# Splitting the last output row of an MLP over two stores, and dropping an early load of gelu's table

## The chip, the cores and the metric

The kernel runs on one core of a Trainium2 chip. A time is the device time of one execution in microseconds. A core has a matrix engine (TensorE, PE in the profile; PEld is its loading of weights), a vector engine (VectorE, DVE), an activation engine (ScalarE, ACT), a general engine (GpSimd, POOL) and a queue engine (SyncE, SP). They run side by side and wait for one another through semaphores. TensorE writes its sums to a memory of its own, PSUM, with eight banks; VectorE and ScalarE move results from there to the on-chip memory SBUF. DMA transfers move data between SBUF and the chip's main memory.

## The reference

The input has 2048 positions of 448 channels. A block computes a long convolution over positions with gates, by Fourier transforms of 4096 points. Then an MLP mixes over the positions, not the channels. Cut to what matters:

```
kv = shift(k) * v
y  = irfft(rfft(pad(kv)) * rfft(pad(ssm_k)))[:S] + kv * ssm_D
h  = x + layernorm(x) * y
z  = layernorm(layernorm(h))
u  = gelu(einsum("bsd,sf->bdf", z, w1) + b1)     # 448 x 1792
out = h + transpose(einsum("bdf,fs->bds", u, w2) + b2)
```

gelu is the tanh form. `w1` is 2048 x 1792 and `w2` is 1792 x 2048, in bf16.

## The kernel before, in words

Position 16 q + r is held in partition q at row r, so that all 2048 positions are 16 rows (R = 16) of 128 partitions by 448 channels. One SBUF tensor, `arena`, holds everything, and one PSUM tensor, `ps`.

The transforms are matmuls with tables of sines. These tables are made in `emit_tables`. VectorE and GpSimd make integer phases, and ScalarE turns them into sines: once 2048 elements a partition for each half of the table `E` (the activation at L823, two times, the first half of the table rows and then the second), and once 384 elements for small factors (L837). At the start a one-element sine (L759) brings sine's table of the activation function into ScalarE. At L851 a one-element gelu reads the small factors' place as a dependence, writes to a scratch column, and has no reader. The compiler puts a load of the function's table (ACT_TABLE_LOAD) ahead of each activation whose function isn't in the table loaded. There are four such loads in the program: ahead of L759 (sine), of L851 (gelu), of the second activation at L823 (sine), and of the first gelu of the MLP at L1270. Between the sines and after them ScalarE also copies sums out of PSUM (L712, L713, L1019).

The stages that follow are, by line: transposes of k and of the filter (L934, L989), the shift of k as matmuls (L953) with the product with v on VectorE (L959), the first stage of both transforms (L1009), its evacuation (L1017, L1019) and a shuffle by DMA (L1025), the second stage (L1044), the products (L1077), the two inverse stages (L1089, L1180), and the gates and both norms (L1187 to L1235).

`emit_mlp` is the MLP. The first layer has 14 groups of 16 matmuls (L1280 for groups 0 to 6, L1290 for 7 to 13), each group followed by a gelu on ScalarE (L1270) that writes `G`, 14 x 448 channels. The second layer has one group for each row r: 14 matmuls with the weights of positions 16 q + r (so the 128 weights of a matmul are 16 elements apart in SBUF) and the 448 columns of `G` (L1300), then a sum of the result, the bias and h on VectorE into `X` (L1304). Stores to the output are issued by SyncE: for rows 0 to 13 in pairs (L1308), for rows 14 and 15 alone (L1311). The table sets the order of the rows: row 14 comes third, row 6 last but one, row 15 last.

TensorE also runs matmuls without a reader, which fill idle time (L979, and L1123 in `emit_warm`). Eight of those stand at the end of its order.

The order of instructions is worked out when the program is built. Each operation is registered with what it reads and writes, an estimated duration and a due time (table `WHEN`). A list scheduler then plays the engines forward: each engine takes the ready operation of the earliest due time, and with equal due times that with the longest way to the end. It also deals out PSUM banks. Each engine then runs its instructions in the order found. Row 15 of the second layer and its sum and store have one due time.

Of the kernel before, what the change touches and what calls it, by code (L numbers as in the profile page):

```python
# [6 lines left out]
ACT = mybir.ActivationFunctionType  # L7
ALU = mybir.AluOpType
# [128 lines left out]
class _Sched:  # L137
# [51 lines left out]
    def op(self, W, fn, r=(), w=(), br=(), bw=(), n=0, kind=None, est=None, dmab=None, keng=16, rate=None, after=(), safter=(), mode=0):  # L189
        if (self.tag, self.t0) != self.step:  # L190
            self.step = (self.tag, self.t0)
            self.count[self.tag] = self.count.get(self.tag, -1) + 1
        o = _Op()
        o.id = len(self.ops)
        o.engs = W if isinstance(W, tuple) else (W,)
        o.eng = None
        o.fn = fn
        o.is_dma = dmab is not None
        o.nbytes = dmab or 0
        o.keng = keng  # L200
        o.lat = 2000.0 + o.nbytes / (22.0 * keng) if o.is_dma else 0.0
        if o.is_dma:
            o.est = {e: (585.0 if e == "pool" else 700.0 if keng == 8 else 460.0) for e in o.engs}
        elif est is not None:
            o.est = dict(est) if isinstance(est, dict) else {e: est for e in o.engs}
        else:
            o.est = {e: self.est_of(e, n, kind) for e in o.engs}
        o.ev = None
        o.mode = mode
        o.t0 = WHEN[self.tag][self.count[self.tag]]  # L210
        if len(o.engs) > 1:
            k = self.flex.get(self.tag, 0)
            self.flex[self.tag] = k + 1
            o.engs = {"a": ("act",), "d": ("dve",), "f": o.engs}[WHERE[self.tag][k]]
        o.rate = rate or (217.0 if keng == 8 else 425.0)
        o.tag = self.tag
        o.acq = []
        o.bufs = []
        o.extra = []
        preds = set(after)  # L220
        spreds = set(safter)
        for spec in r:
            for c in self._cells(spec):
                preds.update(c.w)
                c.r.append(o.id)
        for spec in w:
            g = spec[2] if len(spec) > 2 else None
            for c in self._cells(spec):
                rd = [x for x in c.r if x != o.id]
                if g is not None and c.g == g and not rd:  # L230
                    preds.update(c.gb)
                    c.w.append(o.id)
                else:
                    base = rd if rd else list(c.w)
                    preds.update(base)
                    c.w = [o.id]
                    c.r = []
                    c.g = g
                    c.gb = base
        for b in br:  # L240
            if len(self.ops) and all(self.ops[x].engs == ("pe",) for x in b.writers):
                preds.add(b.writers[-1])
            else:
                preds.update(b.writers)
            b.readers.append(o.id)
            o.bufs.append(b)
            b.users.append(o.id)
        for b in bw:
            if not b.writers:
                o.acq.append(b)  # L250
            else:
                spreds.add(b.writers[-1])
            b.writers.append(o.id)
            o.bufs.append(b)
            b.users.append(o.id)
        preds.discard(o.id)
        spreds -= preds
        o.preds = sorted(preds)
        o.spreds = sorted(spreds)
        self.ops.append(o)  # L260
        return o.id
# [304 lines left out]
def _build(nc, A_q, A_k, A_v, A_shift_k, A_ssm_k, A_ssm_D, B_w1, B_b1, B_w2, B_b2, out):  # L566
# [5 lines left out]
    Bsz, S, D = A_q.shape  # L572
    F = B_w1.shape[1]
    assert Bsz == 1 and S == 2048 and D == 448 and F == 1792 and A_shift_k.shape[-1] == 4
    R = 16
    NFC = F // 128
    EPS = 1e-5
    DB = 2 * D
# [9 lines left out]
    o2d = out[0].rearrange("(q r) d -> q r d", r=R)  # L588
# [15 lines left out]
    o_W2 = (o_TK, o_TU)  # L604
    o_TZ = 132736
    o_TT = o_TZ
    o_WR = 161408
    o_G = o_WR
    o_X = 175744
    o_ET = 190080  # L610
    o_DR = o_ET + 8192
    o_JK = o_DR + 896
# [8 lines left out]
    with ctx:  # L621
        sch = _Sched(nc, ctx, n_dma_sems=112, small_off=SMALL)
        op = sch.op
# [27 lines left out]
        W2 = [view(o, [NFC // 2, S]) for o in o_W2]  # L651
        TZ = view(o_TZ, [R, 2, D])
        G = view(o_G, [NFC, D])
        X = view(o_X, [R, D])
# [7 lines left out]
        JK = view(o_JK, [D])  # L662
# [20 lines left out]
        psum = _Pool(8, pairs=True)  # L683
# [3 lines left out]
        def Pb(b, i=0):  # L687
            return PS[:, b.slots[i], 0:D]
# [32 lines left out]
        def emit_tables():  # L721
# [3 lines left out]
            NB = 3 * 128  # L725
# [7 lines left out]
            o_b = small(16)  # L733
            bias = view(o_b, [4], f32)
            o_pi = o_TT
            o_nb = o_pi + 8 * HALF
            o_sv = o_nb + 4 * NB
# [14 lines left out]
            for x in range(2):  # L752
# [3 lines left out]
                   w=[(o_fr, 512, "fr")], n=128, est=160.0)  # L756
# [3 lines left out]
               w=[(o_JK, 4)], est=1500.0)  # L760
# [3 lines left out]
               n=128, est=190.0)  # L764
# [3 lines left out]
               n=128, est=190.0)  # L768
            op("pool", lambda e, W: e.iota(chi, [[0, 2], [1, 4], [0, 16]], base=0, channel_multiplier=0),
               w=[(o_gc + 512, 512)], n=128, est=190.0)  # L770
            for a, b_, c_ in ((0, 112, 14), (112, 128, 2)):
                op("pool", lambda e, W, a=a, b_=b_, c_=c_: e.iota(gcm[:, a:b_], [[0, 8], [512, c_]], base=512 * 14 * (a > 0),
                                                                 channel_multiplier=0),
                   w=[(o_gc + 1536 + 4 * NB, 512, "gm")], n=128, est=190.0)
                op("pool", lambda e, W, a=a, b_=b_, c_=c_: e.iota(chm[:, a:b_], [[0, 2], [1, 4], [0, c_]], base=0,
                                                                 channel_multiplier=0),
                   w=[(o_gc + 2048 + 4 * NB, 512, "cm")], n=128, est=190.0)
            for k, (b0, st_) in enumerate(((2048, -2048), (2048, 2048), (0, 2048))):
                for a, b_ in (((0, 128),) if k == 0 else ((0, 112), (112, 128))):
                    op("pool", lambda e, W, k=k, b0=b0, st_=st_, a=a, b_=b_: e.iota(  # L780
                        cph[:, 128 * k + a:128 * k + b_], [[st_, 2], [0, (b_ - a) // 2]], base=b0, channel_multiplier=0),
                       w=[(o_gc + 1536 + 512 * k, 512, "cp%d" % k)], n=128, est=190.0)
            sch.t0 = -45.0
            op("dve", lambda e, W: e.tensor_single_scalar(out=ID, in_=idi, scalar=0.0, op=ALU.is_equal),
               r=[(o_gc + 1024, 512)], w=[(o_ID, 256)], n=128)
# [7 lines left out]
            for i, (sh, mk) in enumerate(fields):  # L793
# [3 lines left out]
                                                   op=ALU.logical_shift_right),  # L797
               r=[(o_p, 4), (o_fd, 32)], w=[(o_p + 16, 32)], n=8)
            op("dve", lambda e, W: e.tensor_tensor(out=pc[:, 4:12], in0=pc[:, 4:12], in1=fd[:, 8:16], op=ALU.bitwise_and),
               r=[(o_p + 16, 32), (o_fd + 32, 32)], w=[(o_p + 16, 32)], n=8)  # L800
            for i in (10, 11):
                op("dve", lambda e, W, i=i: e.tensor_tensor(out=pc[:, 4:5], in0=pc[:, 4:5], in1=pc[:, i:i + 1],
                                                            op=ALU.bitwise_or),
                   r=[(o_p + 16, 4), (o_p + 4 * i, 4)], w=[(o_p + 16, 4)], n=1)
            op("dve", lambda e, W: e.tensor_copy(out=pcf[:, 0:6], in_=pc[:, 4:10]), r=[(o_p + 16, 24)],
               w=[(o_p + 48, 24)], n=6)
# [38 lines left out]
            for k, (dst, i) in enumerate(((FW, 0), (MA, 1), (MB, 1))):  # L845
# [2 lines left out]
                   r=[(o_sv + 512 * k, 512), (o_msk + 512 * i, 512)], w=[(o_BD + 256 * k, 256)], n=128, est=460.0)  # L848
            op("pool", lambda e, W: e.tensor_scalar(out=MN, in0=MA, scalar1=-1.0, scalar2=None, op0=ALU.mult),
               r=[(o_BD + 256, 256)], w=[(o_BD + 768, 256)], n=128)  # L850
            op("act", lambda e, W: e.activation(out=JK[:, 0:1], in_=bias[:, 1:2], func=ACT.Gelu_apprx_tanh),  # L851
               r=[(o_b + 4, 4), (o_sv, 4 * NB)], w=[(o_JK, 4)], est=1500.0)

        r_E = lambda r: (o_E + 512 * r, 512)
        r_ET = lambda r: (o_ET + 512 * r, 512)
# [418 lines left out]
        def emit_mlp():  # L1274
            n0 = 7
            bs = [_Buf(psum) for _ in range(n0)]
            for r in range(R):
                sch.t0 = T_M1 + T_DI2 * r
                for fc in range(n0):
                    op("pe", lambda e, W, r=r, fc=fc, b=bs[fc]: e.matmul(  # L1280
                        Pb(b), W1A[:, r, 128 * fc:128 * fc + 128], Q[:, r, :], start=(r == 0), stop=(r == R - 1)),
                       r=[(o_W1A + r * 1792, 1792), (o_Q + r * DB, DB)], bw=[bs[fc]], n=D)
            sch.t0 = T_M1 + 40.0
            for fc in range(n0):
                emit_gelu(bs[fc], fc)
            for fc in range(n0, NFC):
                sch.t0 = T_M1 + 41.0 + 3 * fc
                b = _Buf(psum)
                for r in range(R):
                    op("pe", lambda e, W, r=r, fc=fc, b=b: e.matmul(  # L1290
                        Pb(b), W1B[:, r, 128 * (fc - n0):128 * (fc - n0) + 128], Q[:, r, :], start=(r == 0),
                        stop=(r == R - 1)),
                       r=[(o_W1B + r * 1792, 1792), (o_Q + r * DB, DB)], bw=[b], n=D,
                       safter=i2_last if r == 0 else ())
                emit_gelu(b, fc)
            for r in range(R):
                sch.t0 = T_M1 + 90.0 + 3 * r
                b = _Buf(psum)
                for fc in range(NFC):
                    op("pe", lambda e, W, r=r, fc=fc, b=b: e.matmul(  # L1300
                        Pb(b), W2[fc // 7][:, fc % 7, r:S:R], G[:, fc, :], start=(fc == 0), stop=(fc == NFC - 1)),
                       r=[(o_W2[fc // 7] + fc % 7 * 4096, 4096), (o_G + fc * DB, DB)], bw=[b], n=D)
                A = view(o_TZ + r * 2 * DB, [D], f32)
                op("dve", lambda e, W, r=r, b=b, A=A: e.scalar_tensor_tensor(  # L1304
                    out=X[:, r, :], in0=Pb(b), scalar=bm[:, r:r + 1], in1=A, op0=ALU.add, op1=ALU.add),
                   r=[(o_bm, 64), (o_TZ + r * 2 * DB, 2 * DB)], w=[(o_X + r * DB, DB)], br=[b], n=D, kind="psum")
                if r % 2 == 1 and r < 14:
                    op("sp", lambda e, W, r=r: e.dma_start(o2d[:, r - 1:r + 1, :], X[:, r - 1:r + 1, :]),  # L1308
                       r=[(o_X + (r - 1) * DB, 2 * DB)], dmab=128 * 2 * DB, rate=400.0)
                elif r >= 14:  # L1310
                    op("sp", lambda e, W, r=r: e.dma_start(o2d[:, r:r + 1, :], X[:, r:r + 1, :]),  # L1311
                       r=[(o_X + r * DB, DB)], dmab=128 * DB, rate=400.0)

# [46 lines left out]
```

## Time and profile before

| | us |
|---|---|
| median of 3 runs | 184.91 (184.1 to 185.66) |
| the profiled execution | 185.73 |
| its span, first to last instruction | 183.5 |
| TensorE busy | 172.5 (94%) |
| VectorE busy | 108.1 (59%) |
| ScalarE busy | 92.8 (51%) |
| GpSimd busy | 61.4 (33%) |
| L1300, second layer's matmuls, 224 | 43.9 busy, 353 ns each |
| L1304, the sums after them, 16 | 10.9 busy, 684 ns each |
| ACT_TABLE_LOAD, four, each | 1.28 |

Times in the profile are of one execution; its span leaves out about 2.2 us around the program. The granted TensorE clock was 1.00. A group line has the line, the engine, the operation, what is written and read, the shape and the count, then busy microseconds and the mean nanoseconds of one, then the engine's idle time ahead of the group and what ended it. Matmuls overlap: the 353 ns of one are its length, not the distance to the next. A line of the timeline or of the chain has the start and the length in microseconds, then what ran. In the chain, each piece is what released the next one.

### The profile page before, as it was taken

How to read it: one execution, taken by the hardware profiler on the slowest of the kernel's cores; microseconds unless marked ns; L12 is line 12 of the kernel's file. 1: busy time of each engine (PE TensorE's matmuls, PEld its weight loads, DVE VectorE, ACT ScalarE, POOL GpSimd, SP SyncE). 2: the span in 40 equal slices, each digit the busy share in tenths (PEclk: the TensorE clock that was granted, in tenths of full speed). 3: DMA queues.
4: the chain of work that ended last, by engine and by line, in shares of the span. 5: the costliest groups of instructions: out<-in, count | busy, mean ns of one | idle time of the engine just before them, and what ended most of it. 6: DMA issues, size and time to landing. Idle time of an engine off the chain costs nothing.

```text
span 183.5 us, 3395 instructions
## 1 busy us (share of the span) xinstructions
PE 172.5 (94%) x1331; PEld 98.0 (53%) x1331; DVE 108.1 (59%) x180; ACT 92.8 (51%) x131; POOL 61.4 (33%) x155
## 2 busy tenths in 40 slices
PE   6989999999688898997999899999999999999996
PEld 2777645434233333463545355556556667777773
DVE  7978995897889999996989961000000008222221
ACT  3789877387879998966787473222102020000000
POOL 8053138299310509686788870000000000000000
DMA  6999028579849955777999999300000002011122
GB/s 176 265 377 384 12 100 326 180 261 330 303 138 379 393 207 150 221 206 237 396 405 406 424 416 425 129 0 0 0 4 0 0 0 75 4 50 50 54 96 75
DMA packets 15203, 35.11 MB, mean 191 GB/s; under 512 B 3580, under 2 KB 9244, under 8 KB 15188
## 3 DMA queue, kind: packets, MB, share of 16 engines
q1 hardware_dynamic: 12068, 28.09, 42.1%
q0 software_dynamic: 3072, 6.80, 11.4%
q8 instruction: 10, 0.16, 0.3%
q10 hardware_dynamic: 48, 0.03, 0.1%
q14 instruction: 5, 0.04, 0.1%
HBM read 22.05 MB, written 1.84 MB: 130 GB/s over the span
## 4 chain that ended last, share of the span: by engine, by line
PE 53%; DMA 14%; DVE 14%; ACT 9%; POOL 4%; SPq 3%; issue 3%; DVEq 0%; POOLq 0%
PE ps L1300 23%; PE ps L1290 12%; DMA arena<-arena 8%; PE ps L1280 6%; DMA arena<-in_A_v_dram 6%; ACT arena L712 6%; PE ps L953 4%; DVE arena L1194 3%; PE ps L1089 3%; DVE arena L1019 2%; PE ps L1009 2%; DVE arena L1077 2%; DVE arena L1145 2%; DVE arena L1235 2%; ACT arena L1019 1%
## 5 line engine op out<-in xcount | busy, mean ns | idle before, releaser
L1304 DVE SCALAR_TENSOR_TENSOR arena<-ps,arena 128x448 bf16<-128x448 f32 x16 | 10.9, 684 | 59.4 <-PE ps L1300 59.1
L1300 PE MATMUL ps<-arena 128*128 128x448 bf16 x224 | 43.9, 353 | 0.0
L1300 PEld LDWEIGHTS ps<-arena 128*128 128x128 bf16 x224 | 31.9, 144 | 11.0 <-ACT arena L1270 1.4
L1270 ACT ACTIVATE arena<-ps,arena 128x448 bf16<-128x448 f32 x14 | 8.5, 633 | 32.0 <-PE ps L1290 24.8
L1280 PE MATMUL ps<-arena 128*128 128x448 bf16 x112 | 24.2, 353 | 0.4 <-DVE arena L1235 0.4
L712 ACT CAST arena<-ps 128x896 bf16<-128x896 f32 (+1 forms) x29 | 23.4, 959 | 1.2 <-PE ps L1044 0.7
L1290 PE MATMUL ps<-arena 128*128 128x448 bf16 x112 | 23.3, 352 | 0.0
L1025 POOL DMA_DIRECT2D arena<-arena x32 | 17.6, 554 | 15.2 <-ACT arena L1019 9.3
L1019 ACT CAST arena<-ps 128x896 bf16<-128x896 f32 x17 | 14.7, 910 | 7.1 <-PE ps L1009 7.0
L1044 PE MATMUL ps<-arena 128*64 128x448 bf16 x128 | 14.9, 359 | 2.5 <-DMA arena<-arena 1.2
L712 ACT COPY arena<-ps 128x896 bf16<-128x896 bf16 (+2 forms) x14 | 13.2, 981 | 6.7 <-PE ps L989 3.5
L1280 PEld LDWEIGHTS ps<-arena 128*128 128x128 bf16 x112 | 10.8, 98 | 10.9 <-DVE arena L1235 1.3
L1077 DVE TENSOR_TENSOR arena<-arena 128x1792 bf16<-128x1792 bf16 x16 | 16.5, 1082 | 0.1
L1009 PE MATMUL ps<-arena 128*32 128x448 bf16 x256 | 15.2, 356 | 1.1 <-ACT arena L1019 0.5
L1290 PEld LDWEIGHTS ps<-arena 128*128 128x128 bf16 x112 | 10.9, 98 | 9.9 <-ACT arena L1270 0.2
L1089 PE MATMUL ps<-arena 64*128 64x448 bf16 x128 | 13.9, 352 | 1.7 <-ACT arena L712 1.4
L1113 POOL DMA_DIRECT2D arena<-arena x14 | 8.3, 596 | 16.7 <-ACT arena L712 16.5
L953 PE MATMUL ps<-arena 112*128 112x224 bf16 (+3 forms) x112 | 13.4, 273 | 0.0
L1019 DVE CAST arena<-ps 128x896 bf16<-128x896 f32 x11 | 11.5, 1084 | 0.8 <-PE ps L1009 0.6
L1044 PEld LDWEIGHTS ps<-arena 128*64 128x64 f16 x128 | 5.8, 108 | 11.2 <-ACT arena L712 3.6
L1194 DVE SCALAR_TENSOR_TENSOR arena<-arena 128x448 f32<-128x448 bf16 x16 | 10.6, 674 | 1.8 <-ACT arena L1187 1.7
L953 PEld LDWEIGHTS ps<-arena 112*128 112x128 bf16 x112 | 9.2, 98 | 4.2 <-issue 0.7
(90 smaller groups left out, 207.8 us busy)
## 6 DMA issues: line engine op xcount, KB each, us to landing
arena<-in_B_w_dram SPq DMA_DIRECT2D x8, 896.0 KB, 9.1
arena<-in_B_w_dram SPq DMA_DIRECT2D x2, 2048.0 KB, 16.4
arena<-arena SPq DMA_DIRECT2D x16, 224.0 KB, 4.0
arena<-arena POOLq DMA_DIRECT2D x32, 112.0 KB, 4.0
arena<-in_B_w_dram SPq DMA_DIRECT2D x2, 1536.0 KB, 20.4
arena<-arena POOLq DMA_DIRECT2D x14, 196.0 KB, 5.5
arena<-in_A_ssm_k_dram SPq DMA_DIRECT2D x4, 448.0 KB, 5.2
arena<-in_A_k_dram SPq DMA_DIRECT2D x4, 448.0 KB, 8.5
```

The costliest lines, as they stand in the source:

```text
L712: return e.copy(out=dst(), in_=src())
L953: op("pe", lambda e, W, b=b, i=i, cc=cc, dl=dl, i0=i0, i1=i1, rs=rs, sh=sh: e.matmul(Pb(b, i)[:, 112 * i0:112 * i1 + 112], KX[cc][0:112, i ...
L1009: op("pe", lambda e, W, b=b, r=r, q=q, x=x, c0=c0: e.matmul(PS[32 * q:32 * q + 32, b.slots[x], 0:D], E[:, 2 * r + x, c0:c0 + 32], src[:, r ...
L1019: return e.copy(out=dst, in_=Ppair(b)) if W == "act" else e.tensor_copy(out=dst, in_=Ppair(b))
L1025: shuf[tag].append(op(q_, lambda e, W, g=g, i=i, a=a, nu=nu, jh=jh: e.dma_start(T[a + i:a + i + 4 * nu - 3:4].rearrange("p (j k) c d -> p ...
L1044: op("pe", lambda e, W, b=bs[h], h=h, j=j, c=c, par=par: e.matmul(PS[64 * par:64 * par + 64, b.slots[c], 0:D], FW[:, 64 * c:64 * c + 64], ...
L1077: op("dve", lambda e, W, m=m, i=i: e.tensor_tensor(out=MR(m.slots[0]).rearrange("p (x y) d -> p x y d", x=2), in0=TU[:, i].unsqueeze(2).br ...
L1089: k = op("pe", lambda e, W, b=bs[h], m=ms[h], par=par, t=t, tab=tab, xy=xy, P=P: e.matmul(Pb(b, par), tab[P, :], MR(m.slots[0])[P, xy, :], ...
L1194: return e.scalar_tensor_tensor(out=A, in0=X[:, r, :], scalar=qs[:, r, 0:1], in1=A, op0=ALU.subtract, op1=ALU.mult, **({} if acc is None e ...
L1280: op("pe", lambda e, W, r=r, fc=fc, b=bs[fc]: e.matmul(Pb(b), W1A[:, r, 128 * fc:128 * fc + 128], Q[:, r, :], start=(r == 0), stop=(r == R ...
L1290: op("pe", lambda e, W, r=r, fc=fc, b=b: e.matmul(Pb(b), W1B[:, r, 128 * (fc - n0):128 * (fc - n0) + 128], Q[:, r, :], start=(r == 0), sto ...
L1300: op("pe", lambda e, W, r=r, fc=fc, b=b: e.matmul(Pb(b), W2[fc // 7][:, fc % 7, r:S:R], G[:, fc, :], start=(fc == 0), stop=(fc == NFC - 1) ...
```

## The change

Two things change. In `emit_tables` the one-element gelu is taken away. In `emit_mlp` row 15 of the second layer is computed in two parts, channels 0 to 319 and 320 to 447, each with 14 matmuls, a PSUM bank and a sum of its own. The first part is stored from ScalarE's queue, the second from SyncE's. Rows 0 to 14 keep their form. The lines after L851 move by a few numbers.

```diff
             op("pool", lambda e, W: e.tensor_scalar(out=MN, in0=MA, scalar1=-1.0, scalar2=None, op0=ALU.mult),
                r=[(o_BD + 256, 256)], w=[(o_BD + 768, 256)], n=128)
-            op("act", lambda e, W: e.activation(out=JK[:, 0:1], in_=bias[:, 1:2], func=ACT.Gelu_apprx_tanh),
-               r=[(o_b + 4, 4), (o_sv, 4 * NB)], w=[(o_JK, 4)], est=1500.0)
...
             for r in range(R):
                 sch.t0 = T_M1 + 90.0 + 3 * r
-                b = _Buf(psum)
-                for fc in range(NFC):
-                    op("pe", lambda e, W, r=r, fc=fc, b=b: e.matmul(
-                        Pb(b), W2[fc // 7][:, fc % 7, r:S:R], G[:, fc, :], start=(fc == 0), stop=(fc == NFC - 1)),
-                       r=[(o_W2[fc // 7] + fc % 7 * 4096, 4096), (o_G + fc * DB, DB)], bw=[b], n=D)
                 A = view(o_TZ + r * 2 * DB, [D], f32)
-                op("dve", lambda e, W, r=r, b=b, A=A: e.scalar_tensor_tensor(
-                    out=X[:, r, :], in0=Pb(b), scalar=bm[:, r:r + 1], in1=A, op0=ALU.add, op1=ALU.add),
-                   r=[(o_bm, 64), (o_TZ + r * 2 * DB, 2 * DB)], w=[(o_X + r * DB, DB)], br=[b], n=D, kind="psum")
+                for d0, d1 in ((0, D),) if r < R - 1 else ((0, 320), (320, D)):
+                    b = _Buf(psum)
+                    for fc in range(NFC):
+                        op("pe", lambda e, W, r=r, fc=fc, b=b, d0=d0, d1=d1: e.matmul(
+                            Pb(b)[:, d0:d1], W2[fc // 7][:, fc % 7, r:S:R], G[:, fc, d0:d1], start=(fc == 0), stop=(fc == NFC - 1)),
+                           r=[(o_W2[fc // 7] + fc % 7 * 4096, 4096), (o_G + fc * DB, DB)], bw=[b], n=d1 - d0)
+                    op("dve", lambda e, W, r=r, b=b, A=A, d0=d0, d1=d1: e.scalar_tensor_tensor(
+                        out=X[:, r, d0:d1], in0=Pb(b)[:, d0:d1], scalar=bm[:, r:r + 1], in1=A[:, d0:d1], op0=ALU.add, op1=ALU.add),
+                       r=[(o_bm, 64), (o_TZ + r * 2 * DB, 2 * DB)], w=[(o_X + r * DB + 2 * d0, 2 * (d1 - d0))], br=[b],
+                       n=d1 - d0, kind="psum")
+                    if r == R - 1:
+                        op("sp" if d0 else "act", lambda e, W, r=r, d0=d0, d1=d1: e.dma_start(o2d[:, r:r + 1, d0:d1], X[:, r:r + 1, d0:d1]),
+                           r=[(o_X + r * DB + 2 * d0, 2 * (d1 - d0))], dmab=128 * 2 * (d1 - d0), rate=400.0)
                 if r % 2 == 1 and r < 14:
                     op("sp", lambda e, W, r=r: e.dma_start(o2d[:, r - 1:r + 1, :], X[:, r - 1:r + 1, :]),
                        r=[(o_X + (r - 1) * DB, 2 * DB)], dmab=128 * 2 * DB, rate=400.0)
-                elif r >= 14:
+                elif r == R - 2:
                     op("sp", lambda e, W, r=r: e.dma_start(o2d[:, r:r + 1, :], X[:, r:r + 1, :]),
                        r=[(o_X + r * DB, DB)], dmab=128 * DB, rate=400.0)
```

## The prediction

> **What bounds the kernel now.** I read the page's chain first, then the same chain in order of time around the two places that the diff touches, then ScalarE's and TensorE's timelines there. The page's chain:
>
> ```profile
> PE 53%; DMA 14%; DVE 14%; ACT 9%; POOL 4%; SPq 3%; issue 3%; DVEq 0%; POOLq 0%
> ...
> L1304 DVE SCALAR_TENSOR_TENSOR arena<-ps,arena 128x448 bf16<-128x448 f32 x16 | 10.9, 684 | 59.4 <-PE ps L1300 59.1
> L1300 PE MATMUL ps<-arena 128*128 128x448 bf16 x224 | 43.9, 353 | 0.0
> ```
>
> TensorE is half of the path. In the last layer (L1300) it never idles, and VectorE waits for it. The chain in order of time, at its end:
>
> ```profile
> 149.62 31.03 PE ps L1300 x164
> 180.65 1.51 PE ps L1123 x8
> ```
>
> 164 matmuls in 31.03 us: one 448-column matmul each 189 ns. The eight at L1123 are fillers with no reader; they end at 182.17. The timeline of the last 6 us shows what really ends last:
>
> ```profile
> 180.69 0.68 DVE L1304 SCALAR_TENSOR_TENSOR arena<-ps,arena 128x448 bf16<-128x448 f32 x1 [1.97 <-PE ps L1300]
> 181.40 0.33 SPq L1311 DMA_DIRECT2D out_dram<-arena  x1
> ```
>
> The last matmul ends at 180.65, its sum takes 0.68, SyncE issues the store at 181.40. L1311's stores take 1.7 us from issue to landing (1.66 for this one), so it lands at about 183.06, and 0.48 of closing waits make the span of 183.54. After the last matmul there are thus 2.9 us in series. The other place, ScalarE's timeline:
>
> ```profile
> 16.56 0.90 ACT L712 COPY arena<-ps 128x896 bf16<-128x896 bf16 x1
> 17.47 1.28 ACT L851 ACT_TABLE_LOAD   x1
> 18.76 0.20 ACT L851 ACTIVATE arena<-arena 128x1 bf16<-128x1 f32 x1
> 18.99 1.28 ACT L823 ACT_TABLE_LOAD   x1
> 20.28 2.00 ACT L823 ACTIVATE arena<-arena 128x2048 f16<-128x2048 int32 x1
> 22.91 1.01 ACT L712 COPY arena<-ps 112x1024 bf16<-112x1024 bf16 x1 [0.62 <-PE ps L934]
> ```
>
> and the chain over the same time:
>
> ```profile
> 6.41 11.67 DMA arena<-in_A_v_dram
> ...
> 18.17 1.10 DVE arena L959
> ...
> 19.32 0.56 PE ps L1009 x8
> 19.88 2.54 PE ps L953 x23
> 22.42 0.45 PE ps L934 x8
> 22.87 1.53 PE ps L953 x14
> 24.40 0.60 PE ps L1009 x8
> ```
>
> The chain goes load of V, VectorE's product, then TensorE without a gap from 19.32 to 25.00. ScalarE isn't on it. After its sine ScalarE waits 0.62 us and then 1.10 us more for TensorE.
>
> [...]
>
> **Part 1: the warm-up gelu.** It takes from ScalarE all from 17.47 to 20.28: two table loads and a one-element activation, 2.81 us. The second sine then ends near 19.5. What is late next is the copy that began at 22.91: it waits for the eight transposes at L934, which stand in TensorE's order behind 23 matmuls that VectorE released. So 2.81 us becomes idle time: 0.62 becomes about 3.4. The readers of this sine's table (the matmuls of later rows in the first stage) come after 25 us. Gain taken: 0, between 0 and 2.81. The waits of TensorE for ScalarE between 15 and 30 us sum to 0.2. If the cover (TensorE's run to 25.00) were gone, up to 1.7 us would show. In the built program ScalarE's loads go from four to two, and the one ahead of the first gelu stays. In the trace it runs at 108.5 and the first gelu then still waits 2.03 us for TensorE: nothing changes there.
>
> **Part 2: the last row.** The order on TensorE is the same up to row 15, whose 14 matmuls become 28: eleven of 320 columns, then both widths mixed, and seven of 128 columns last. The bank for the 128 columns waits for the sum of the row ahead of it (178.04 to 178.72); it is asked for at 177.84 + 11 x 0.135 = 179.3, so no stall. Row 15 starts at 180.65 - 0.35 - 13 x 0.189 = 177.84.
> A 320-column matmul scaled from 189 is 135 ns. For 128 columns with a strided weight load the nearest row is L989, whose weights have the same step of 16 elements:
>
> ```profile
> 9.81 1.20 PE L989 MATMUL ps<-arena 112*128 112x112 bf16 x16 [0.69 <-DMA arena<-in_A_ssm_k_dram]
> 10.85 0.61 PE L934 MATMUL ps<-arena 128*112 128x128 bf16 x8
> ```
>
> (1.20 - 0.24) / 15 = 64 ns apart at 112 columns, though one load lasts 157: loads overlap. L934, 128 columns from contiguous weights, gives (0.61 - 0.22) / 7 = 56. I take 65 for 128 columns; the ends are 56 and 144, the length of one weight load at L1300.
> The row: 14 x 135 + 14 x 65 = 2.80 us against 14 x 189 = 2.65. The last matmul starts at 177.84 + 14 x 0.135 + 13 x 0.065 = 180.58 and lasts 0.22 (L934) instead of 0.35: it ends at 180.80, 0.15 later.
> The sums: the last 320-column matmul starts at 177.84 + 13 x 0.135 + 7 x 0.065 = 180.05, lasts 0.31 (as L953 at 336 columns), and the first sum runs from 180.40 for 684 - 128 x 1.04 = 551 ns, to 180.95. The second needs 684 - 320 x 1.04 = 351 ns. It is ready at 180.84 but stands behind the first on VectorE; successive sums there overlap by some 0.08 (three of 1084 ns at L1019 take 3.10), so it runs from 180.87 to 181.22. Before: 181.37. Gain 0.15.
> The stores: 224 KB took 1.9 us, 112 KB 1.66, so 32 KB would take 1.66 - 80 x 0.0022 = 1.48. For rows of 256 bytes the ends are 1.48 and 1.9; I take 1.6. SyncE's store lands at 181.22 + 0.03 + 1.6 = 182.85, 0.2 earlier than before. The other 80 KB leave ScalarE's queue at 180.98, where nothing is queued behind them, and land by 182.6 at 1.6 us. ScalarE's issue is the unknown: at L1102 one took 694 ns, SyncE's 672, but another 1517 while SyncE issued too.
> Sum: 0.2 us less, of 183.5 + 2.2 = 185.7 us of the profiled execution. The median is 184.91, 0.8 below that execution, and I put the difference on it: 184.7.
>
> **The rivals.** *The loads were on the path*: 184.91 - 2.81 - 0.2 = 181.9. For it: 2.81 us between two sines that the transforms need. Against: the two waits after the sine. Chance 0.06.
> *Weight loads pace the narrow matmuls* (slower): if a strided load doesn't hide behind 128 columns, each of the 28 takes 144 ns. The last matmul then ends at 177.84 + 27 x 0.144 + 0.22 = 181.95, 1.30 late; the shorter sum gives back 0.33, the store 0.06 to 0.2: about 0.85 worse, 185.8. It decides from a pitch p with 177.84 + 1.89 + 13 p + 0.22 - 180.65 = 0.42 (0.33 from the sum, 0.09 from the store), so 86 ns. [...] Against: L989's 64. Chance 0.12.
> *ScalarE's store lands last*: an issue of 1.52 us in place of 0.33 puts 182.6 to 183.8, 0.7 worse, 185.6. Chance 0.07.
> *The forecast*: between 0.4 less and no change. Chance 0.75. That the change doesn't do what it says is out: the program has it.
>
> **How the numbers follow.** The three runs spread from 184.1 to 185.66, so about 1% is what a measurement of this kernel tells from no change. Only the first rival crosses it by itself. Both slower ones stay within it, and need the runs' spread to cross. Faster 0.08, same 0.86, slower 0.06. The range of 183.7 to 185.9 takes in the two slower rivals and the forecast with the spread of the median, and leaves the first rival out.
>
> **What would show it.** ScalarE: no load between 17 and 20 us, and its next copy still near 22.9 after a wait for TensorE of about 3.4 us. Row 15: 28 matmuls in 2.8 us; 4.0 would make the second rival right. Two sums of about 0.55 and 0.35 us back to back, the last ending near 181.2. Two stores, SyncE's landing last, near 182.85. I am wrong if TensorE's run from 19.32 starts or ends earlier than before, since then ScalarE held it, or if the narrow pitch is above 86 ns.

## The result, and the profile after

The changed kernel takes 184.62 us (median of 20 runs) and the kernel before 185.38 (20 runs beside them). The ratio is 0.998, with a 95% interval of 0.9958 to 1.0003: between 0.8 us less and 0.1 us more, so an unchanged time isn't excluded. The ratio leaves out one run of each kernel that was over 1.5% slower than that kernel's fastest, and it isn't the quotient of the two medians, which is 0.996. The profiled execution took 184.68 us, with a span of 182.5 (before 185.73 and 183.5).

ScalarE around the place of the removed gelu, as a timeline of the changed kernel (start, length, what ran, in brackets the idle time ahead and its releaser):

```profile
16.25 0.90 ACT L712 COPY arena<-ps 128x896 bf16<-128x896 bf16 x1
17.03 2.01 ACT L823 ACTIVATE arena<-arena 128x2048 f16<-128x2048 int32 x1
22.16 1.01 ACT L712 COPY arena<-ps 112x1024 bf16<-112x1024 bf16 x1 [3.11 <-PE ps L932]
24.27 2.52 ACT L1017 CAST arena<-ps 128x896 bf16<-128x896 f32 x3 [1.10 <-PE ps L1007]
```

The second sine now follows the copy directly and starts at 17.03 instead of 20.28. The next copy does not follow it: ScalarE waits 3.11 us for the transposes (L932 is the former L934), where it waited 0.62. The time won is idle time.

The chain over the same stretch, in order of time:

```profile
3.96 7.81 DMA arena<-in_A_k_dram
...
17.88 1.25 PE ps L1007 x24
19.13 2.54 PE ps L951 x23
21.67 0.45 PE ps L932 x8
22.12 1.53 PE ps L951 x14
23.65 0.60 PE ps L1007 x8
```

From 19.13 on these are the steps and lengths of before, each some 0.75 us earlier. But they no longer wait for the load of V and its product; the chain goes back to the load of k through TensorE alone.

The end of the kernel, as a timeline:

```profile
177.31 0.68 DVE L1303 SCALAR_TENSOR_TENSOR arena<-ps,arena 128x448 bf16<-128x448 f32 x1 [1.97 <-PE ps L1300]
178.02 0.33 SPq L1311 DMA_DIRECT2D out_dram<-arena  x1
179.65 0.81 DVE L1303 SCALAR_TENSOR_TENSOR arena<-ps,arena 128x320 bf16<-128x320 f32 x2 [1.66 <-PE ps L1300]
...
179.88 1.68 PE L1121 MATMUL ps<-arena 128*128 128x448 f16 x8
180.24 0.38 ACTq L1308 DMA_DIRECT2D out_dram<-arena  x1
180.49 0.33 SPq L1308 DMA_DIRECT2D out_dram<-arena  x1
```

and the groups by shape:

```profile
L1303 DVE SCALAR_TENSOR_TENSOR arena<-ps,arena 128x320 bf16<-128x320 f32 x1 | 0.6, 550 | 1.7 <-PE ps L1300 1.7
...
L1303 DVE SCALAR_TENSOR_TENSOR arena<-ps,arena 128x128 bf16<-128x128 f32 x1 | 0.3, 341 | 0.0
```

I count from the start of the last full row's sum, 177.31 here and 178.04 before. Up to there the second layer is the same in both. SyncE's last store is issued 3.18 us after it (before 181.40 - 178.04 = 3.36). It lands 1.55 us later by the trace (before 1.66), and 0.48 us of closing waits follow in both. The end is thus at 5.21 us against 5.50: 0.18 from the earlier issue and 0.11 from the shorter landing, 0.29 in all. ScalarE's store lands at 180.24 + 1.63 = 181.87, ahead of SyncE's at 182.04.

The profiled span is 1.02 us shorter, and three stretches share that out. Up to ScalarE's first cast (L1017, the former L1019) it is 24.27 against 25.02 us, so 0.75 less. From there to the start of the last gelu of the MLP it is 124.65 and 124.63, so nothing in these two profiles. From that gelu to the end it is 33.59 and 33.88, so 0.29 less. The two gelus, changed kernel and then before:

```profile
148.93 0.64 ACT L1268 ACTIVATE arena<-ps,arena 128x448 bf16<-128x448 f32 x1 [2.39 <-PE ps L1288]
```

```profile
149.66 0.63 ACT L1270 ACTIVATE arena<-ps,arena 128x448 bf16<-128x448 f32 x1 [2.39 <-PE ps L1290]
```

The stretch after the last gelu is a good ruler for this change. It is 33.88 us in all four profiles below that keep row 15 whole (the kernel before and three others), and 33.59 and 33.60 in the two that split it as the change does. The front of the kernel is no such ruler: it follows the input loads. Nor is the stretch between: it takes from 124.04 to 124.89 us in the eight profiles without added table loads.

### The profile page after: what moved, and what is told of

The parts are those of the page before. It is cut to its first block, busy times and chain, and to the rows that moved or that the text cites. A ratio compares the mean times of both kernels' runs of the same rounds, so it can differ in the third digit from the quotient of the medians.

```text
span 182.5 us, 3423 instructions
## 1 busy us (share of the span) xinstructions
PE 172.1 (94%) x1345; PEld 98.7 (54%) x1345; DVE 108.3 (59%) x181; ACT 89.8 (49%) x128; POOL 61.4 (34%) x155
## 4 chain that ended last, share of the span: by engine, by line
PE 58%; DVE 10%; DMA 10%; ACT 9%; POOL 7%; issue 2%; SPq 2%; POOLq 0%
PE ps L1300 23%; PE ps L1288 12%; PE ps L1278 7%; ACT arena L712 6%; PE ps L951 6%; DMA arena<-arena 5%; DMA arena<-in_A_k_dram 4%; POOL arena L1023 4%; DVE arena L1192 3%; PE ps L1007 3%; PE ps L1087 3%; PE ps L932 2%; ACT arena L1017 2%; DVE arena L1075 2%; DVE arena L1143 2%
## 5 line engine op out<-in xcount | busy, mean ns | idle before, releaser
L1303 DVE SCALAR_TENSOR_TENSOR arena<-ps,arena 128x448 bf16<-128x448 f32 (+2 forms) x17 | 11.1, 656 | 59.1 <-PE ps L1300 58.8
L1300 PE MATMUL ps<-arena 128*128 128x448 bf16 (+2 forms) x238 | 44.0, 342 | 0.0
L1300 PEld LDWEIGHTS ps<-arena 128*128 128x128 bf16 x238 | 32.8, 145 | 10.4 <-ACT arena L1268 1.4
L1278 PE MATMUL ps<-arena 128*128 128x448 bf16 x112 | 24.2, 353 | 0.4 <-DVE arena L1233 0.4
L1288 PE MATMUL ps<-arena 128*128 128x448 bf16 x112 | 23.3, 352 | 0.0
L1017 ACT CAST arena<-ps 128x896 bf16<-128x896 f32 x17 | 14.6, 910 | 7.0 <-PE ps L1007 7.0
L1278 PEld LDWEIGHTS ps<-arena 128*128 128x128 bf16 x112 | 10.8, 98 | 10.9 <-DVE arena L1233 1.3
L1288 PEld LDWEIGHTS ps<-arena 128*128 128x128 bf16 x112 | 10.9, 98 | 9.9 <-ACT arena L1268 0.2
L1017 DVE CAST arena<-ps 128x896 bf16<-128x896 f32 x11 | 11.6, 1086 | 0.7 <-PE ps L1007 0.6
```

What stands on the lines that cost most here:

```text
L1017: return e.copy(out=dst, in_=Ppair(b)) if W == "act" else e.tensor_copy(out=dst, in_=Ppair(b))
L1278: op("pe", lambda e, W, r=r, fc=fc, b=bs[fc]: e.matmul(Pb(b), W1A[:, r, 128 * fc:128 * fc + 128], Q[:, r, :], start=(r == 0), stop=(r == R ...
L1288: op("pe", lambda e, W, r=r, fc=fc, b=b: e.matmul(Pb(b), W1B[:, r, 128 * (fc - n0):128 * (fc - n0) + 128], Q[:, r, :], start=(r == 0), sto ...
L1300: op("pe", lambda e, W, r=r, fc=fc, b=b, d0=d0, d1=d1: e.matmul(Pb(b)[:, d0:d1], W2[fc // 7][:, fc % 7, r:S:R], G[:, fc, d0:d1], start=(fc ...
```

## The experiments

### The split alone

The changed kernel with the gelu put back.

```diff
+            op("act", lambda e, W: e.activation(out=JK[:, 0:1], in_=bias[:, 1:2], func=ACT.Gelu_apprx_tanh),
+               r=[(o_b + 4, 4), (o_sv, 4 * NB)], w=[(o_JK, 4)], est=1500.0)
```

> The changed kernel with the one-element gelu put back: the split row alone. If the table loads lay in idle time (my theory), this is as fast as the changed kernel: 0.3 us under the kernel before (ratio 0.998), and from the start of the last full row's sum to the end of the span 5.2 us, against 5.5 before. If the gain came from the loads (the rival), the ratio is 1.000.

Measured: 184.82 us, ratio 0.9987 (0.9964 to 1.0009). From the last gelu to the end it takes 33.60 us, from the last full row's sum 5.22. The time alone doesn't tell this from no gain. The saving at the end, 0.28 in the trace, belongs to the split. ScalarE's timeline of this kernel shows the front with the loads kept:

```profile
20.25 2.00 ACT L823 ACTIVATE arena<-arena 128x2048 f16<-128x2048 int32 x1
22.43 1.01 ACT L712 COPY arena<-ps 112x1024 bf16<-112x1024 bf16 x1 [0.18 <-PE ps L934]
24.54 2.52 ACT L1019 CAST arena<-ps 128x896 bf16<-128x896 f32 x3 [1.10 <-PE ps L1009]
```

The sine is as late as in the kernel before (20.25 and 20.28), yet the first cast starts at 24.54, 0.48 earlier than before. The chain of this profile also goes through the load of k and TensorE without V:

```profile
3.95 8.10 DMA arena<-in_A_k_dram
...
12.09 1.10 PE ps L934 x16
...
23.92 0.60 PE ps L1009 x8
```

So an early front comes without any removal of loads. The 0.27 us by which the cast is still later than in the changed kernel (24.54 against 24.27) is the 0.27 by which TensorE starts later behind the load of k (12.09 against 11.82).

### The gelu alone

The kernel before without the one-element gelu.

```diff
-            op("act", lambda e, W: e.activation(out=JK[:, 0:1], in_=bias[:, 1:2], func=ACT.Gelu_apprx_tanh),
-               r=[(o_b + 4, 4), (o_sv, 4 * NB)], w=[(o_JK, 4)], est=1500.0)
```

> The kernel before without the one-element gelu: row 15 whole. My theory: ratio 1.000, ScalarE waits about 3.1 us for TensorE after the second sine in place of 0.62, and the last sum to the end of the span stays as before (2.85 us). The rival (loads on the path): up to 2.8 us less, ratio 0.985, or at least the 0.998 of the whole change.

Measured: 184.99 us, ratio 0.9996 (0.9975 to 1.0018), so between 0.46 us less and 0.33 more. The 2.81 us of ScalarE's time were not on the path. The time doesn't exclude a small gain, such as the ratio of 0.998 that the weaker rival names; there the trace has to decide. Its timeline:

```profile
16.75 2.01 ACT L823 ACTIVATE arena<-arena 128x2048 f16<-128x2048 int32 x1
22.25 1.01 ACT L712 COPY arena<-ps 112x1024 bf16<-112x1024 bf16 x1 [3.49 <-PE ps L932]
24.37 2.52 ACT L1017 CAST arena<-ps 128x896 bf16<-128x896 f32 x3 [1.10 <-PE ps L1007]
```

The wait after the sine is 3.49 us. From the last gelu to the end it is 33.88, as before. In this profile the chain does pass over the product with v, and its first cast still starts at 24.37. TensorE's run behind the product begins with

```profile
18.66 0.56 PE ps L1007 x8
```

and the cast follows 5.71 us after that start, as it follows 5.70 after 19.32 in the kernel before. The first cast starts between 24.10 and 24.56 us in the six profiles without the loads (the changed kernel, this one, and four below) and at 24.54 and 25.02 in the two with them. In six of these eight the chain goes over the product with v, and the cast follows TensorE's start behind it by 5.70 or 5.71 us; in the other two, the changed kernel and the split alone, it goes over the load of k, and the cast follows TensorE's start behind that by 12.45 us. Each of the two distances is the same with the loads and without them. So what moves the first cast is the arrival of v and k, and not ScalarE.

### One table switch more, and two more

The gelu's place gets one (or two) more pairs of a one-element gelu and a one-element sine. Each pair adds two loads, 2.81 us of ScalarE's time ahead of the second sine.

```diff
-            op("act", lambda e, W: e.activation(out=JK[:, 0:1], in_=bias[:, 1:2], func=ACT.Gelu_apprx_tanh),
-               r=[(o_b + 4, 4), (o_sv, 4 * NB)], w=[(o_JK, 4)], est=1500.0)
+            def warm_tables(e, W):
+                for i in range(1):
+                    e.activation(out=JK[:, 8 * i + 8:8 * i + 9], in_=bias[:, 1:2], func=ACT.Gelu_apprx_tanh)
+                    e.activation(out=JK[:, 8 * i + 12:8 * i + 13], in_=bias[:, 1:2], func=ACT.Sin)
+                return e.activation(out=JK[:, 0:1], in_=bias[:, 1:2], func=ACT.Gelu_apprx_tanh)
+            op("act", warm_tables, r=[(o_b + 4, 4), (o_sv, 4 * NB)], w=[(o_JK, 4)], est=1500.0)
```

(with `range(2)` in the second kernel)

> The kernel before with two more table loads and two more one-element activations ahead of the second sine, 2.81 us more. My theory of a cover: the copy after the sine starts near 25.1 in place of 22.9, it ends at 26.1, and the first cast, at 25.02 before, becomes late by 1.0 to 1.1 us: the kernel is 1.1 us slower (ratio 1.006). If ScalarE were on the path before: 2.8 us slower (1.015). If later stages had slack for it: 1.000.

> Four more loads, 5.62 us more ahead of the second sine. With the cover used up by the first 1.7 us, each further one counts in full: 3.9 us slower (ratio 1.021), 2.8 more than with one pair. On the path from the start: 5.6 (1.030). Slack in later stages: less than 3.9.

Measured for one pair: 186.83 us, ratio 1.0096 (1.0064 to 1.0128), which is 1.2 to 2.4 us more with 1.8 in the middle. Neither 2.8 us (loads on the path from the start) nor nothing (slack later on) lies in that interval; the 1.1 expected lies just under it. ScalarE's timeline:

```profile
22.17 1.28 ACT L823 ACT_TABLE_LOAD   x1
23.46 2.00 ACT L823 ACTIVATE arena<-arena 128x2048 f16<-128x2048 int32 x1
25.37 0.99 ACT L712 COPY arena<-ps 112x1024 bf16<-112x1024 bf16 x1
26.26 2.56 ACT L1023 CAST arena<-ps 128x896 bf16<-128x896 f32 x3
```

The copy and the cast stand right behind the sine now, without a wait: ScalarE has come onto the path. From the copy ahead of the loads to the first cast it takes 26.26 - 16.73 = 9.53 us, against 25.02 - 16.56 = 8.46 before: 1.07 more, near the 1.09 that 2.81 less a cover of 1.72 gives. The time lost more. What may add to it is that the cover isn't the same in each execution. It is the two waits after the sine: 0.62 + 1.10 = 1.72 in the kernel before's profile, but 0.18 + 1.10 = 1.28 in the profile of the split alone, with the same loads in ScalarE's order. With the smaller cover, one pair costs 1.53. How often each occurs was not measured, and the stretch from the cast to the last gelu moves as well (124.24 us here). So it is shown that the added loads cost less than their length, and more than nothing; the rest of the 1.8 us stays open.

Measured for two pairs: 191.02 us, ratio 1.0312 (1.0265 to 1.0359), 5.8 us more. The expected 3.9 was missed. By the time alone, the rival with the loads on the path from the start (5.6) would fit; the run with one pair has ruled it out, and the trace has another source. The same distance is now 28.27 - 15.72 = 12.55 us, 4.09 more than before, near the 3.90 of 5.62 - 1.72. The rest lies behind it. TensorE, by its timeline with two pairs:

```profile
28.42 4.49 PE L1013 MATMUL ps<-arena 128*32 128x448 bf16 x56 [4.24 <-ACT arena L712]
```

and in stretches (length, busy time and count of TensorE, its weight loads, VectorE, ScalarE and GpSimd, then the granted clock, the DMA share and GB/s):

```profile
24.20:28.40 4.20, 0.00 (x0) 0.00 (x0) 0.62 (x1) 4.19 (x4) 0.63 (x1) 1.00 0.00 0
28.41:31.82 3.41, 3.40 (x40) 1.51 (x44) 1.19 (x2) 2.51 (x3) 1.86 (x5) 0.50 0.40 159
31.82:36.00 4.18, 4.18 (x64) 2.16 (x57) 2.38 (x3) 3.39 (x5) 2.79 (x6) 1.00 0.75 296
```

TensorE stood idle for 4.24 us, and after that its clock was granted at 0.50 for 3.41 us. The 56 matmuls behind the wait took 4.49 us. With one pair the same 56 stand behind a wait of 1.45 us, the clock there is granted at 1.00, and they take 3.16 us:

```profile
26.41 3.16 PE L1013 MATMUL ps<-arena 128*32 128x448 bf16 x56 [1.45 <-ACT arena L712]
```

So the same matmuls take 1.33 us longer after the long wait. From the first cast to the last gelu it takes 125.97 us, which is 1.33 more than the 124.63 before, and 1.1 to 1.9 more than in the eight profiles without added loads. 4.09 + 1.33 is 5.4, inside the interval's 4.9 to 6.6.

### Seven split rows

Rows 1, 11, 12, 3, 0 and 6 are split like row 15: six more rows of 28 matmuls.

```diff
-                for d0, d1 in ((0, D),) if r < R - 1 else ((0, 320), (320, D)):
+                for d0, d1 in ((0, D),) if r not in (1, 11, 12, 3, 0, 6, 15) else ((0, 320), (320, D)):
```

> The changed kernel with the last seven rows of the second layer split in 320 and 128 channels, not one: 84 more matmuls. With weight loads that overlap (my pitch of 65 ns for 128 columns), each split row takes 2.78 to 2.80 us in place of 2.65: 6 x 0.14 = 0.8 us more than the changed kernel, 0.5 more than before (ratio 1.003). If a strided weight load paced the narrow matmuls (144 ns), 6 x 1.4 = 8.3 us more (1.044). [...]

Measured: 185.85 us, ratio 1.0064 (1.0038 to 1.0091), 0.7 to 1.7 us more than the kernel before. The sums of two split rows in VectorE's timeline:

```profile
174.82 0.81 DVE L1303 SCALAR_TENSOR_TENSOR arena<-ps,arena 128x320 bf16<-128x320 f32 x2 [1.98 <-PE ps L1300]
177.61 0.81 DVE L1303 SCALAR_TENSOR_TENSOR arena<-ps,arena 128x320 bf16<-128x320 f32 x2 [1.98 <-PE ps L1300]
```

They are 2.79 us apart, where full rows are 2.65 apart (178.04 to 180.69 before). A split row costs TensorE 0.14 us, so the narrow matmuls come about every 64 ns if the 320-column ones take 135. Paced by 144 ns each, a row would take 4.03. From the last gelu to the end it takes 34.44 us, 0.85 more than with one split row, which is six times 0.14. That is 0.56 more than before, a little below what the time shows at the least (0.70). The rest of the 1.2 us is in no view of this one profile, and stays open.

### Both stores on SyncE

```diff
-                        op("sp" if d0 else "act", lambda e, W, r=r, d0=d0, d1=d1: e.dma_start(o2d[:, r:r + 1, d0:d1], X[:, r:r + 1, d0:d1]),
+                        op("sp", lambda e, W, r=r, d0=d0, d1=d1: e.dma_start(o2d[:, r:r + 1, d0:d1], X[:, r:r + 1, d0:d1]),
```

> The changed kernel with both stores of row 15 issued by SyncE. My theory: the second queue saves at most what is left of the first store's issue of 0.33 us; the second store leaves about 0.07 us later, and from the start of the last full row's sum to the end of the span it is 5.26 us against 5.19. If the second queue carried the gain: 5.5, as before the change.

Measured: 184.3 us in a single execution, span 182.1. SyncE, in the timeline of the end:

```profile
179.16 0.81 DVE L1303 SCALAR_TENSOR_TENSOR arena<-ps,arena 128x320 bf16<-128x320 f32 x2 [1.66 <-PE ps L1300]
...
179.74 0.81 SPq L1308 DMA_DIRECT2D out_dram<-arena  x2
```

From the start of the first issue to the end of the second it is 0.81 us, where one issue alone takes 332 ns in the trace. From the last full row's sum to the end it is 5.32 us, 0.11 more than with two queues (5.26 was expected). The second queue is worth that much.

### One store for both parts

The order of the matmuls and the two sums stay as in the changed kernel (written out by hand, since the scheduler would choose another); row 15 is stored once, whole, by SyncE.

```diff
-                    if r == R - 1:
-                        op("sp" if d0 else "act", lambda e, W, r=r, d0=d0, d1=d1: e.dma_start(o2d[:, r:r + 1, d0:d1], X[:, r:r + 1, d0:d1]),
-                           r=[(o_X + r * DB + 2 * d0, 2 * (d1 - d0))], dmab=128 * 2 * (d1 - d0), rate=400.0)
...
-                elif r == R - 2:
+                elif r >= R - 2:
```

> The changed kernel with the matmuls in the same order and the two sums, but one store of all 448 channels by SyncE. The sums give 0.2 of the tail's 0.3 us, the smaller last store 0.1: 5.30 us from the start of the last full row's sum to the end of the span, 1.66 of it from issue to landing in place of 1.55. If the gain lay in the stores: 5.5.

Measured: 184.6 us in a single execution, span 182.4. The end:

```profile
179.46 0.81 DVE L1311 SCALAR_TENSOR_TENSOR arena<-ps,arena 128x320 bf16<-128x320 f32 x2 [1.66 <-PE ps L1306]
...
180.30 0.33 SPq L1319 DMA_DIRECT2D out_dram<-arena  x1
```

SyncE issues 180.30 - 177.12 = 3.18 us after the last full row's sum, as in the changed kernel, and the store takes 1.66 to land, as before. From that sum to the end it is 5.32: the split of the computation saves 0.18, and the split of the store the other 0.11. The two add up to the 0.29. The end is also the 5.32 us of two stores on one queue: there the last store lands 0.11 us sooner than a whole one, but is issued 0.12 later. So splitting the store gains only together with the second queue. These are single profiles, compared by their distance from the last full row's sum, which agrees within 0.01 us in profiles with the same ending.

### The parts one after the other, 288 and 160 channels

In the change, the second sum is ready while the first still runs. Here all matmuls of the first part stand ahead of those of the second, and the cut is moved so that the first sum is done in time.

```diff
-                for d0, d1 in ((0, D),) if r < R - 1 else ((0, 320), (320, D)):
+                parts = ((0, D),) if r < R - 1 else ((0, 288), (288, D))
...
+                seq = [(0, fc) for fc in range(NFC)] if r < R - 1 else [(x, fc) for x in (0, 1) for fc in range(NFC)]
```

> A version meant to beat the changed kernel: 288 and 160 channels, all matmuls of the first part ahead of those of the second. Row 15 takes 14 x (122 + 69) = 2.68 us in place of 2.78, the last sum is 0.04 longer but never stands behind the first: about 0.08 us less, 5.1 us from the start of the last full row's sum to the end. That is under what the runs can tell; ratio to the kernel before 0.998. If narrower last parts are what counts (the store or the sum), it is slower than the changed kernel.

Measured: 184.84 us, ratio 0.9995 (0.9974 to 1.0017). The end:

```profile
178.90 0.52 DVE L1309 SCALAR_TENSOR_TENSOR arena<-ps,arena 128x288 bf16<-128x288 f32 x1 [1.03 <-PE ps L1304]
179.45 0.38 ACTq L1314 DMA_DIRECT2D out_dram<-arena  x1
...
179.88 0.38 DVE L1309 SCALAR_TENSOR_TENSOR arena<-ps,arena 128x160 bf16<-128x160 f32 x1 [0.46 <-PE ps L1304]
180.29 0.33 SPq L1314 DMA_DIRECT2D out_dram<-arena  x1
```

The first sum is over long before the second is due, and VectorE waits 0.46 us for TensorE between them. From the last full row's sum (177.19) to the end it is 5.08 us, 0.13 less than in the changed kernel and 0.42 less than before (5.1 was expected). Some 0.08 of the 0.13 is the earlier issue, 3.10 us after that sum, and 0.05 the landing, 1.50 us from issue, although the store is the larger one (40 KB, and 32 in the changed kernel); why it lands sooner isn't shown. In the time this can't be told from nothing.

## Why the prediction was right, point by point

The forecast was 184.7 us and no difference that a measurement can tell; 184.62 and a ratio of 0.998 came out. That 184.62 lies so near is in part luck. The forecast started from 184.91, a median of three runs, while other medians of the same kernel are 185.38 (20 runs), 185.0 (39 runs on one chip) and 184.72 (24 on another): they differ by more than the whole change is worth. What holds is the small difference, and it rests on the steps below. The prediction's 1% for what can be told was too wide for so many runs, whose interval spans 0.45%, but that interval holds no difference too.

*Part 1, gain 0.* Right, by the time of the gelu alone (0.9996, at most 0.46 us gained) and by the first cast, which keeps its distance from the inputs with the loads and without. The named step, a wait growing from 0.62 to about 3.4 us, is seen as 3.11 in the changed kernel and 3.49 with the gelu alone. The prediction's sign of being wrong, a run of TensorE that ends earlier, did occur (24.25 against 25.00). It was a bad sign to name. With the loads kept, that run also ends early, at 24.52 in the chain of the split alone, because its beginning follows the input loads: both ends of the run are 0.27 us later than in the changed kernel. Also too sure was the cover: 1.7 us is one profile's, and 1.28 stood in another with the same loads.

*Part 2, the row.* 2.80 us were predicted. The last full row's sum and the first filler matmul behind row 15 are 179.88 - 177.31 = 2.57 us apart, against 180.49 - 178.04 = 2.45 before, so row 15 takes about 2.65 + 0.12 = 2.77; the seven split rows give 2.79. The sums of 551 and 351 ns came as 550 and 341, the second behind the first as said. The prediction names no trace for the slope of 1.04 ns a column behind those two figures; in the changed kernel's trace the sums of 448, 320 and 128 columns (684, 550 and 341 ns) give 1.05 and 1.09.

*Part 2, the stores.* SyncE's landing of 1.6 us was 1.55. ScalarE's issue, the unknown, took 0.38 us, and its store landed 0.17 ahead of the other. The forecast sum was 0.2 us less; the trace has 0.29, of which 0.18 was put at 0.15 and 0.11 at 0.06.

*The rivals.* The loads on the path, 181.9: fell with the gelu alone. Weight loads that pace the narrow matmuls: fell with a row of 2.79 us, a pitch of about 64 ns, well under the 86 from which it would decide. ScalarE's store last: fell with its issue of 0.38 us.

## What to carry to other kernels

Time taken from an engine that isn't on the chain became a longer wait right behind it (0.62 us before, 3.11 after). Before counting a gain, read the wait that follows; before adding work there, remember that this wait is a margin that moves from one execution to the next (0.62 us in one profile, 0.18 in another with the same loads). At the very end of a kernel, where nothing overlaps, cutting the last tile shortened the last sum and, with a second queue, the last store, but here all of it was 0.3 us of 185; a stretch of the trace measured from a fixed event shows such a gain where the time can't.

## What the runs showed of the hardware that was not expected

- A stall cost TensorE more than its length. With two pairs, after 4.24 us idle, the clock was granted at 0.50 for 3.41 us, and the 56 matmuls that followed took 4.49 us in place of 3.16. With one pair, where TensorE stood idle for 1.45 us, the clock stayed at 1.00 (1.000 in the mean of that run, against 0.991 with two pairs). From what length on a wait is followed by a slower clock, these two runs don't show.
- Small stores landed after nearly the same time, whatever their rows: 1.66 us from issue for 896 bytes a partition, 1.63 for 640, 1.55 for 256, and 1.50 for 320. 1792 bytes took 1.9. The shortest rows were not the fastest.
- Two stores that SyncE issued one behind the other took 0.81 us from the start of the first issue to the end of the second; one issue alone took 332 ns, so two would be 0.66.
